# The opening loads of a cross-covariance attention and MLP kernel: the first chunks of k and q in two half transfers, the second chunks over GpSimd's queue

## The chip, the cores and the metric

The kernel runs on one core of one Trainium2 chip; the other cores are idle. Its time is the device time of one execution in microseconds (us), the median of several runs. A core has five engines that run side by side: TensorE (PE, matrix multiply), VectorE (DVE), ScalarE (ACT), GpSimd (POOL) and SyncE (SP). SP, ACT and POOL can also issue DMA transfers; each has a queue of its own, and all queues are served by the same 16 DMA engines.

## The reference

Inputs are q, k and v, each of shape (4, 6080, 256) in float32, and the weights of an MLP. For each of the four batches:

```python
qn = q / (np.linalg.norm(q, axis=1, keepdims=True) + 1e-06)
kn = k / (np.linalg.norm(k, axis=1, keepdims=True) + 1e-06)
s = kn.transpose(0, 2, 1) @ qn / tau        # 256 x 256
a = softmax(s)                              # over the last axis
x = v @ a
h = x @ w_in                                # 256 -> 2048
r = np.maximum(h, 0.0)
out = (s_moe * (r * r) + b_moe) @ w_out     # 2048 -> 256
```

The output is 24320 x 256 in float32. The sum over the 6080 rows has to be complete before the softmax of a batch can be taken, so no output row of a batch can be computed before all of that batch's k and q have been read.

## The kernel before

**The two parts.** For each batch the kernel forms the Gram matrix of q and k (256 x 256, in the PSUM tile `s_ps`, line 148), the column sums of squares of k and q (`n_ps`, lines 246 and 250), from these the softmax (`eT`, line 302), and folds the softmax into w_in (`wa`, lines 323 to 332). Then groups of 512 tokens run through the MLP: `mm1` (line 755), relu, square, and the second product (lines 802, 830 and 926). For batches 1 to 3 the first part is spread over the steps of the MLP of the batch before, so it runs beside other work. For batch 0 there is nothing to run beside: this is the opening of the kernel, about its first 37 us, and the change is in it.

**The opening.** The rows of k and q of batch 0 are cut into 13 chunks: 11 of 512 rows (128 partitions, 4 rows each, 512 KB in float32 for k and the same for q), one of 256 rows and one of 192. A chunk's tile `qk` holds both in float16. There are two ways into it:

- The first `NDIRECT` = 2 chunks come as float32 over the queues of SP (k) and ACT (q) into `raw32` (line 130), and are then cast into `qk` by DVE (k, line 138) and ACT (q, line 139).
- The other chunks come over GpSimd's queue (line 132), whose transfers cast to float16 on the way. The pool `qk_pool` has 8 buffers, and a transfer of this queue waits until the one issued eight transfers earlier has landed.

The loads are issued in the order of the chunks (lines 498 to 510): k and q of each, for the last three chunks (`NLATE` = 3) first all of k and then all of q. After them on GpSimd's queue come the first rows of v, the weights, and so on.

**The work on a chunk.** TensorE does 8 matmuls of 128x256 for a chunk (line 148), which need k and q. ACT squares k, and q of odd chunks (line 179); DVE squares q of even chunks (line 176) and folds the squares into one running sum (lines 193 and 207). After some chunks TensorE also does one or two matmuls on constant data whose result nobody reads:

```python
FILL = {-8: 1, -7: 1, -6: 1, -5: 2, -4: 2}   # key: chunk minus 13
def keep_busy(n):
    for _ in range(n):
        po(nc.tensor.matmul(h_tile("idle_ps")[:, 0, :], fill[:, :P], fill, ...
```

So chunks 5, 6 and 7 are followed by one such filler and chunks 8 and 9 by two. For the last three chunks the order is another: first the squares and the norm of k, then ACT's four steps from the sum of squares to 1/norm (line 271), and beside them the squares, norms and matmuls of q. Then `scale`, the exponentials, and the first block of `wa`, after which the first matmul of line 755 can start.

**What sets the order.** Nearly every instruction goes through `po`, which keeps it in the order of the program on its engine; so the order on each engine is that of the source. The transfers of line 130 are not under `po`, but in the compiled program they are the first that SP and ACT issue.

Of the kernel before, what the change touches and what calls it, by code (L numbers as in the profile page):

```python
# [16 lines left out]
def kernel(  # L17
# [12 lines left out]
    nc = tc.nc  # L30
    P = 128
# [23 lines left out]
    def po(ins):  # L55

        tc.keep_in_program_order(ins)
        return ins
# [34 lines left out]


    JC = 4
    NDIRECT = 2

    def make_chunks(rows_of):
        chunks, at = [], 0
# [11 lines left out]
    class Gram:  # L111
# [7 lines left out]
        def load(self, c, parts=(0, 1)):  # L119

            at, np_, jc = self.chunks[c]
            if 0 in parts:
                self.raw[c] = qk_pool.tile([P, 2, JC, C], FP16, tag="qk", name="qk")
            t = self.raw[c]
            direct = self.b == 0 and c < NDIRECT
            for i in parts:
                src = (k, q)[i]
                rows = src[self.b, at : at + np_ * jc, :].rearrange("(p j) c -> p j c", j=jc)
                if direct:
                    (nc.sync, nc.scalar)[i].dma_start(out=raw32[:, c, i], in_=rows)  # L130
                else:
                    po(nc.gpsimd.dma_start(out=t[:np_, i, :jc, :], in_=rows))
            self.tiles[c] = t[:, 1], t[:, 0]
# [354 lines left out]
    g0 = grams[0]  # L488
    raw32 = gpool.tile([P, NDIRECT, 2, JC, C], FP32, tag="g16", name="raw32")

# [6 lines left out]
    po(nc.vector.tensor_copy(out=ones_id, in_=fill.bitcast(FP32)[:, :P]))  # L497
    for c in range(NDIRECT):
        g0.load(c)
        g0.cast(c)  # L500
    for c in range(NDIRECT, len(g0.chunks) - NLATE):
        g0.load(c)
        if c == NDIRECT:
            po(nc.gpsimd.affine_select(
                out=ident16, in_=ones_id, compare_op=ALU.is_equal, fill=0.0, base=0,
# [156 lines left out]
    for i, f in enumerate(folds):  # L662
        early.setdefault(FOLDS[i], []).append(f)
    at_step(14, lambda: po(nc.vector.tensor_scalar_mul(
        out=s_out, in0=s_bc, scalar1=1.0 / (LAM * LAM))))
# [357 lines left out]
```

## Time and profile before

| | |
|---|---|
| time, median of 3 runs | 714.04 us (714.01 to 714.29) |
| span in the profile | 712.5 us |
| TensorE busy | 691.5 us, 97% |
| DVE, ACT, POOL busy | 635.2, 548.5, 113.4 us |
| GpSimd's DMA queue, q0 | 43.74 MB, 38.2% of 16 engines |
| SP's and ACT's queues, q1 and q10 | 37.71 MB, 21.9%; 1.25 MB, 0.5% |
| chain that ended last | PE 95%, DMA 3%, ACT 1%, DVE 1% |

The busy shares are averages over the whole span. The chain of waits starts from the last instruction and goes back, at each step, to what released it; its shares say which engine the end of the kernel hung on. In lines of the timeline the first number is the start in us from the beginning of the span, the second the length, then engine, source line, operation, what it writes and reads, and how often; in brackets stands how long the engine was idle before and what ended that. In lines of the chain there is the start, the length and the piece of work. In the DMA view one digit stands for a slice of the stretch, 9 for 90% or more of the 16 engines' time; GB/s are the bytes moved, for a casting transfer those written.

### The profile page before, as it was taken

Reading aid. Unit: us, or ns where it says so; the run is one execution under the profiler, and the core shown is the slowest. Engines: PE = TensorE matmul, PEld = TensorE weight load, DVE = VectorE, ACT = ScalarE, POOL = GpSimd, SP = SyncE. Lnnn points to the kernel's source line nnn. Section 1 sums busy time; section 2 is a strip of 40 time slices with the busy share of each in tenths; the row PEclk is TensorE's granted clock in tenths of the full one; section 3 lists DMA queues with packets and bytes.
Section 4 is the critical chain, followed back from the end, with each engine's and each line's share of the span. In section 5 each row is a group of like instructions: output and inputs, shape, how many; then the busy total and the mean of one; then the engine's idle time right before and its main releaser. Section 6 shows DMA issues by size and latency. Waiting matters only on the chain.

```text
span 712.5 us, 17529 instructions
## 1 busy us (share of the span) xinstructions
PE 691.5 (97%) x7422; PEld 501.7 (70%) x7422; DVE 635.2 (89%) x906; ACT 548.5 (77%) x599; POOL 113.4 (16%) x191
## 2 busy tenths in 40 slices
PE   4699999999999999999999999999999999999998
PEld 2456777776777777777677777777768777777777
DVE  4889999999988989998999899998998888888886
ACT  5789877787787777778877777777876777777875
POOL 4533132202101222111010222111000000000000
DMA  9999998556665878455762888737433333321202
GB/s 233 207 258 174 175 168 140 112 103 121 119 123 105 138 139 147 106 92 104 153 127 52 149 137 146 130 76 97 100 65 75 94 71 75 97 61 46 83 31 75
DMA packets 87838, 83.81 MB, mean 118 GB/s; under 512 B 56352, under 2 KB 62768, under 8 KB 87760
## 3 DMA queue, kind: packets, MB, share of 16 engines
q0 software_dynamic: 26992, 43.74, 38.2%
q1 hardware_dynamic: 60192, 37.71, 21.9%
q8 instruction: 58, 0.95, 0.6%
q10 hardware_dynamic: 576, 1.25, 0.5%
q14 instruction: 20, 0.16, 0.1%
HBM read 78.91 MB, written 24.90 MB: 146 GB/s over the span
## 4 chain that ended last, share of the span: by engine, by line
PE 95%; DMA 3%; ACT 1%; DVE 1%; issue 0%; DVEq 0%; ACTq 0%
PE h_ps L755 46%; PE o_ps L926 40%; PE s_ps L148 4%; DMA qk<-in_k_dram 1%; PE wa_ps L388 1%; DMA raw<-in_q_dram 1%; PE o_ps L830 1%; ACT sq L179 1%; PE o_ps L802 0%; PE wa_ps L330 0%; DVE f L193 0%; ACT r L271 0%; PE n_ps L246 0%; ACT qk L139 0%; DVE f L207 0%
## 5 line engine op out<-in xcount | busy, mean ns | idle before, releaser
L765 ACT ACTIVATE r<-h_ps 128x1024 f16<-128x1024 f32 (+1 forms) x384 | 388.4, 1013 | 144.2 <-PE h_ps L755 140.6
L755 PE MATMUL h_ps<-vT,wa 128*128 128x512 f16 (+7 forms) x1632 | 452.1, 364 | 0.5 <-ACT wa L323 0.5
L926 PEld LDWEIGHTS <-S 128*128 128x128 f16 x2944 | 198.1, 98 | 84.3
L926 PEld LDWEIGHTS <-g 128*128 128x128 f16 x2208 | 155.0, 98 | 74.1
L778 DVE TENSOR_TENSOR g<-r 128x2048 f16<-128x2048 f16 (+2 forms) x150 | 174.4, 1163 | 10.1 <-ACT r L765 9.7
L926 PE MATMUL o_ps<-T,S 128*128 128x128 f16 x2208 | 183.1, 219 | 0.0
L755 PEld LDWEIGHTS <-wa 128*128 128x128 f16 x1632 | 136.5, 98 | 19.0 <-ACT wa L323 1.0
L926 PE MATMUL o_ps<-w_out,g 128*128 128x128 f16 x1472 | 134.2, 219 | 0.0
L776 ACT ACTIVATE g<-r 128x1024 f16<-128x1024 f16 (+1 forms) x97 | 100.3, 1034 | 0.2
L783 DVE SCALAR_TENSOR_TENSOR o_sb<-o_ps,s_out,u 128x256 f32<-128x256 f32 x138 | 66.2, 480 | 36.1 <-PE o_ps L926 34.5
L148 PE MATMUL s_ps<-qk 128*128 128x256 f16 (+1 forms) x384 | 70.1, 283 | 16.0 <-ACT qk L139 9.3
L452 POOL DMA_DIRECT2D v<-in_v_dram x48 | 31.3, 661 | 241.1 <-DMA vT<-v 165.1
L209 POOL DMA_DIRECT2D f<-f x33 | 28.8, 874 | 245.6 <-DVE f L193 202.8
L783 DVE SCALAR_TENSOR_TENSOR u<-o_ps,s_out,rowconst 128x256 f32<-128x256 f32 x138 | 65.7, 476 | 0.0
L926 PE MATMUL o_ps<-w_out,S 128*128 128x128 f16 x736 | 63.5, 219 | 0.0
L926 PE MATMUL o_ps<-N,g 128*128 128x128 f16 x736 | 63.4, 219 | 0.0
L855 DVE TENSOR_TENSOR S<-S,g 128x2048 f16<-128x2048 f16 (+1 forms) x47 | 56.4, 1201 | 1.2
L179 ACT ACTIVATE sq<-qk 128x1024 f16<-128x1024 f16 (+2 forms) x53 | 54.5, 1041 | 3.9 <-DMA qk<-in_k_dram 2.3
L853 DVE TENSOR_TENSOR S<-g 128x2048 f16<-128x2048 f16 (+1 forms) x47 | 56.0, 1192 | 0.0
L857 DVE TENSOR_TENSOR S<-g 128x2048 f16<-128x2048 f16 x46 | 55.8, 1214 | 0.0
L859 DVE TENSOR_TENSOR S<-g,S 128x2048 f16<-128x2048 f16 x46 | 55.8, 1214 | 0.0
L148 PEld LDWEIGHTS <-qk 128*128 128x128 f16 (+1 forms) x384 | 32.2, 101 | 21.4 <-ACT qk L139 9.8
(103 smaller groups left out, 333.6 us busy)
## 6 DMA issues: line engine op xcount, KB each, us to landing
out_dram<-o_sb SPq DMA_DIRECT2D x43, 512.0 KB, 2.9
v<-in_v_dram POOLq DMA_DIRECT2D x47, 256.0 KB, 4.8
qk<-in_k_dram POOLq DMA_DIRECT2D x42, 256.0 KB, 6.5
qk<-in_q_dram POOLq DMA_DIRECT2D x42, 256.0 KB, 7.5
f<-f POOLq DMA_DIRECT2D x30, 128.0 KB, 3.1
vT<-v SPq DMA_TRANSPOSE x182, 3.2
w<-in_moe_w_out_dram POOLq DMA_DIRECT2D x4, 512.0 KB, 9.8
out_dram<-o_sb SPq DMA_DIRECT2D x8, 256.0 KB, 5.1
```

What stands on the lines that cost most here:

```text
L148: po(nc.tensor.matmul(self.s_ps[:, ch, :], qc[:np_, j, ts(ch, P)], kc[:np_, j, :], start=(c == 0 and j == 0 and ch == 0), stop=(c == len(s ...
L179: po(nc.scalar.activation(out=st["sq"][:np_, a, js, :], in_=(qc, kc)[a][:np_, js, :], func=AF.Square))
L755: po(nc.tensor.matmul(dst, wa[:, ci, ts(m, P)], src, start=(ci == 0), stop=(ci == CH - 1), skip_group_check=True))
L765: po(nc.scalar.activation(out=r16[:, :, i % 2, :n], in_=h_tiles.pop((g, i))[:, :, :n], func=AF.Relu))
L776: po(nc.scalar.activation(out=dst, in_=src, func=AF.Square))
L778: po(nc.vector.tensor_mul(dst, src, src))
L783: po(nc.vector.scalar_tensor_tensor(out=dst, in0=src, scalar=s_out, op0=ALU.mult, in1=add, op1=ALU.add))
L853: po(nc.vector.tensor_add(T[1], A21, A22))
L855: po(nc.vector.tensor_sub(T[2], T[1], A11))
L857: po(nc.vector.tensor_sub(T[3], A11, A21))
L859: po(nc.vector.tensor_sub(T[4], A12, T[2]))
L926: po(nc.tensor.matmul(st[name][:, j, :], a()[:, i, ts(j, P)], w[:, i, :], start=first, stop=last, skip_group_check=True))
```

## The change

`NDIRECT` goes from 2 to 1, so only chunk 0 still takes the way over `raw32`, and chunk 1 goes over GpSimd's queue with its cast on the way. The transfers of chunk 0 are cut into two of 64 partitions each, one behind the other on SP's queue for k and on ACT's for q. It is for having the first data early with less in front of it, and for taking the casts of chunk 1 off DVE and ACT.

```diff
-    NDIRECT = 2
+    NDIRECT = 1
...
                 if direct:
-                    (nc.sync, nc.scalar)[i].dma_start(out=raw32[:, c, i], in_=rows)
+                    for h in range(2):
+                        ps = ts(h, P // 2)
+                        (nc.sync, nc.scalar)[i].dma_start(out=raw32[ps, c, i], in_=rows[ps])
                 else:
                     po(nc.gpsimd.dma_start(out=t[:np_, i, :jc, :], in_=rows))
```

In the compiled program TensorE, DVE, ACT and SP keep their order. DVE and ACT each lose one cast (lines 138 and 139), SP and ACT issue two transfers of 64 x 1024 in place of two of 128 x 1024, and GpSimd issues two more of 128 x 1024, chunk 1 now being the first on its queue. The semaphores that GpSimd's transfers report to are counted on by two places.

## The prediction

> **What bounds the kernel now.** I read the page first (engine shares, slices, chain), then the chain of the opening in order of time, then the DMA view and TensorE's timeline of the opening alone. TensorE is busy 97% of the span and the chain is 95% TensorE, so from about 37.5 us to the end an edit to two early loads can't do more than shift everything. The opening is different. The chain of waits from 26 to 38 us:
>
> ```profile
> 20.68 9.46 DMA qk<-in_k_dram
> 30.13 0.02 issue
> 30.16 1.07 ACT sq L179
> 31.22 0.02 issue
> 31.25 0.44 DVE half L223
> 31.68 0.04 issue
> 31.73 0.95 PE n_ps L246 x7
> 32.68 0.02 issue
> 32.70 0.48 ACT r L271
> ```
>
> The reader sees that the first matmuls of the output (L755, 37.49 us) hang on the landing of k's chunk 10 at 30.13 us, and then on a string of short steps with no slack. What sets that landing is the DMA view of 10 to 30 us (slices of 0.5 us; GB/s counts the written fp16, so bytes read are twice that):
>
> ```profile
> DMA  9999999999999999999999999999999999999999
> GB/s 209 213 217 201 205 213 209 213 209 205 213 209 205 213 205 213 209 209 213 205 209 209 213 209 209 209 205 213 213 209 205 201 217 217 205 209 201 217 197 197
> ...
> q0 software_dynamic: 2372, 4.17, 112.4%
> ```
>
> All 16 engines are full, by GpSimd's queue (q0) alone: 4.17 MB written, 8.34 MB read in 20 us, 417 GB/s. k and q of batch 0 are 2 x 6080 x 256 x 4 B = 12.45 MB, that is 29.9 us at this rate, counted back from a last landing of about 32.5 us or a little later. So the opening is a stream of a fixed number of bytes, and its end depends on when the engines fill up and on nothing else. TensorE's timeline of the opening shows the pace:
>
> ```profile
> 7.45 1.89 PE L148 MATMUL s_ps<-qk 128*128 128x256 f16 x8 [7.45 <-ACT qk L139]
> 11.24 1.04 PE L148 MATMUL s_ps<-qk 128*128 128x256 f16 x4 [1.90 <-ACT qk L139]
> ```
>
> ```profile
> 11.24 4.66 PE L148 MATMUL s_ps<-qk 128*128 128x256 f16 x24 [1.90 <-ACT qk L139]
> 16.38 1.05 PE L148 MATMUL s_ps<-qk 128*128 128x256 f16 x8 [0.48 <-DMA qk<-in_q_dram]
> 18.93 1.05 PE L148 MATMUL s_ps<-qk 128*128 128x256 f16 x8 [1.51 <-DMA qk<-in_q_dram]
> ...
> 26.40 1.05 PE L148 MATMUL s_ps<-qk 128*128 128x256 f16 x8 [1.17 <-DMA qk<-in_q_dram]
> 27.20 0.71 PE L548 MATMUL idle_ps<-fill 128*128 128x512 f32 x2
> 28.95 1.05 PE L148 MATMUL s_ps<-qk 128*128 128x256 f16 x8 [1.04 <-DMA qk<-in_q_dram]
> ```
>
> Chunk 0 runs at 7.45. Chunk 1 waits for its casts until 11.24, and by then chunks 2 and 3 are in, so three chunks run as one block of 24. From chunk 4 on, each waits for its own q, 2.51 us apart ((28.95 - 16.38) / 5). TensorE, DVE and ACT are behind at 11 us and have caught up by 17.
>
> **What the Trainium skill says.** "DMA: Bandwidth & Descriptors", section "Rules for kernel authors": two transfers to the two partition halves serialise, since both spray across all 16 engines, and spreading issues over SP, ACT and GpSimd brings no bandwidth. The trace can't show halves; on spreading it agrees: with three queues at work (5.4 to 9.8 us) 1.44 MB were written, 0.39 of them cast, so 1.83 MB read in 4.4 us, 416 GB/s against 417 later with one queue. The same page, "Why a DMA increments its semaphore by 16 and not by 1": the engines used are the largest number up to 16 that divides the slowest dimension, so 64 partitions still use 16. No trace here shows it; I rely on it. Same page, "Queues, rings and completion order": an engine goes round-robin between its rings. It agrees: of 5.4 to 9.8 us SP's ring had about 0.49 MB, ACT's 0.56 and GpSimd's read 0.78. "TensorE: Matmul & The Clock Gate", Part 1: TensorE runs at half clock until some 3.4 us of sustained activity, in free-running windows. It agrees: the 8 matmuls of chunk 0 start (1.89 - 0.42) / 7 = 0.21 us apart (0.42 is the length of one there), those of chunk 4 (1.05 - 0.27) / 7 = 0.11. In the block of 24, 23 steps take 4.66 - 0.27 = 4.39 us, which is 18 at 0.213 and 5 at 0.109: the clock rose about 3.85 us after 11.24.
>
> **The change, part by part.**
> (1) Chunk 0 in halves: still two issues on SP and two on ACT (0.40 to 0.45 us each, the same count as the two whole chunks of before), the same 1.05 MB, the same casts, which wait for both halves. Bounds: if a half's issue takes half as long, 0.2 us are gained on the second half; if each transfer had its own ramp, 0.2 to 0.4 us lost on chunk 0. Both only move chunk 0's landing (6.17 and 6.35 us now), which nothing at 30 us waits for. I take 0.
> (2) Chunk 1 goes over q0: two DMA instructions more on GpSimd (0.53 to 0.58 us each, beside a stream that takes 1.25 us per transfer: hidden), and one cast less on DVE (0.69 us) and ACT (1.04). Those two engines wait for DMA from 17 us on, so 0 at the end.
> (3) When the engines are full. By 5.4 us SP's and ACT's rings had moved 0.56 + 0.49 = 1.05 MB, just the size of chunk 0, and q0 its first packet at 5.45, though issued at 1.30. In the changed kernel the two rings hold only chunk 0, so they run dry just when q0 starts. Is there a hole? By the packet records chunk 0's transfers end on the 16 engines between 4.98 and 5.96 us, and q0's first packets follow in the same order of engines, 0.5 to 0.6 us behind each: they look held by their turn, not by arrival. With an empty queue later in the kernel, v's loads show 0.8 to 1.24 us from issue to first packet. If they are held by turn, no hole; if 5.45 is the arrival, up to 0.46 us on the fastest engine and none on the slowest, which ends at 5.96 and alone decides a landing. I take 0, bound +0.46.
> (4) Depth. q0 keeps 8 transfers in flight: each issue waits for the one 8 before. With two more at the head, chunk 8's k still waits for chunk 4's k, chunk 10's k for chunk 6's: the later waits are the same, renumbered, and what is queued behind them on GpSimd moves with them. Only chunk 5 now waits for chunk 1 (about 8 us), with seven transfers (8.8 us of work) before it: hidden.
> (5) Rate: 1.05 MB read through q0 instead of mixed rings: 417 against 416 GB/s, 0.01 us.
> (6) TensorE's pattern. The n-th transfer of 512 KB lets its matmuls start at 16.38 - 1.255 x (10 - n). So chunk 1 (n = 4) can run at 8.85, chunk 2 at 11.36, chunk 3 at 13.87. At half clock a chunk takes 8 x 0.213 = 1.71 us: 7.45 to 9.16, 9.16 to 10.87, 11.36 to 13.07, 13.87 to 15.58. The block of 24 is gone, so the clock may rise later. Up to chunk 7 that costs nothing: 1.71 plus a filler of 0.43 is 2.14 of 2.51 us. Chunks 8 and 9 with two fillers are 2.56 each, so TensorE is busy without a break from 26.40 to 31.5 and the clock should be up by 30 to 33. Cost 0 if up by 31.7.
>
> Sum: 0 + 0 + 0 + 0 + 0 + 0, so 714.0 us, the present median, and nothing after 37.5 us changes.
>
> **The rivals.**
> A, slower: the half clock lasts into the late phase. For it: the lost block; the fillers were sized for an array already at speed. Against: 5.1 us without a break just before. If it lasts until about 33.2, the 7 norm matmuls from 31.73 take 1.49 in place of 0.95 us and chunk 10 begins 0.67 us late: 714.7. If it lasts through, chunks 10 to 12 and q's norms add to 37.5 in place of 34.92: +2.6, 716.6.
> B, faster: the engines fill earlier. First data is at 1.83 us and the slices reach full rate near 4. The 1.05 MB of 5.4 us are worth 2.5 us at 417 GB/s, an effective start of 2.9; perfect from 1.83 would be 1.1 us better, 712.9, the ceiling. The spread of 0.98 us between engines lasts; halves could even it out: half of it is 0.5 us, 713.5. Against: nothing in the change shortens the first packet's way.
> C: a hole or a slower ramp by smaller transfers, the bounds of (1) and (3): +0.5, 714.5.
>
> **How the numbers follow.** No change within 0.4 us: 0.67. A: 0.11 at 714.7 and 0.05 at 716.6. B: 0.12, of which 0.03 beyond what I reckon and past 0.2%. C: 0.05. The limit of 0.2% is 1.43 us: below 712.6 only the tail of B (0.03, and 0.01 for what I don't see), above 715.5 only the worse half of A (0.05, and 0.03 for what I don't see). Range 713.4 to 715.0: it takes in A's likelier value, most of B and C, and leaves out A's worse value, B's end and the unseen, about 0.15.
>
> **What would show it.** Right: chunk 1's matmuls start near 9 and not at 11.24 and its cast is gone; q0 runs from about 5 us or before with the DMA slices full; chunks 4 to 9 start within 0.3 us of 16.38 to 28.95; chunk 10's k lands within 0.4 us of 30.13; L755 starts within 0.4 us of 37.49; the L148 matmuls of chunk 10 are 0.11 us apart. Wrong: those matmuls at 0.21 us apart (A); an empty slice between 4 and 7 us with all landings later (C); landings all earlier by over 0.5 us (B); or a difference that arises after 38 us, which none of my steps has.

## The result, and the profile after

| | before | after |
|---|---|---|
| time, median of 22 runs each | 714.11 us (713.79 to 714.39) | 715.19 us (714.96 to 715.99) |
| ratio, 95% interval | | 1.0016 (1.001 to 1.0023) |
| ACT starts the square of k's chunk 10 | 30.16 us | 31.25 us |
| first matmul of line 755 (757 after) | 37.49 us | 38.66 us |

The changed kernel is 1.1 us slower; the forecast was no change, in a range that ended at 715.0. Line numbers from the loads on are two higher after the change. The chain of waits of the changed kernel from 20 to 40 us:

```profile
21.77 9.46 DMA qk<-in_k_dram
31.22 0.02 issue
31.25 1.07 ACT sq L181
...
32.81 0.95 PE n_ps L248 x7
...
33.79 0.48 ACT r L273
...
38.66 0.61 PE h_ps L757 x2
```

The reader sees the same chain with the same lengths, every piece 1.1 us later (the first matmul 1.17; the two profiled runs, 715.36 and 714.21 us, are 1.15 apart). Nothing is added behind the landing of k's chunk 10, so the loss lies before it. The DMA view of the changed kernel from 10 to 30 us:

```profile
DMA packets 2301, 4.19 MB, mean 209 GB/s; under 512 B 256, under 2 KB 256, under 8 KB 2301
...
q0 software_dynamic: 2301, 4.19, 112.2%
```

That is the rate of before (4.17 MB). So the loss is older than 10 us. The view of 4 to 9 us has it. A queue's line gives its packets, the MB written, and the time that the packets took as a share of 16 engines' time. First the kernel before:

```profile
DMA  9998999989999899999999999999999999999999
...
DMA packets 558, 1.84 MB, mean 367 GB/s; under 512 B 50, under 2 KB 50, under 8 KB 558
...
q10 hardware_dynamic: 224, 0.83, 40.7%
q1 hardware_dynamic: 212, 0.77, 39.1%
q0 software_dynamic: 122, 0.24, 25.7%
```

and the changed kernel:

```profile
DMA  9499999999999999999999969799699899999998
...
DMA packets 477, 1.13 MB, mean 226 GB/s; under 512 B 73, under 2 KB 73, under 8 KB 477
...
q0 software_dynamic: 282, 0.53, 56.9%
q10 hardware_dynamic: 115, 0.34, 32.0%
q1 hardware_dynamic: 80, 0.26, 18.6%
```

q0 reads twice what it writes, so before 1.84 + 0.24 = 2.08 MB were read in these 5 us, after 1.13 + 0.53 = 1.66. The 0.42 MB that are missing take 1.0 us at 417 GB/s: the whole loss. Yet the slices are nearly full in both, and the three queues' shares add up to 105.5% before and 107.5% after (a sum past 100% means that the times of packets overlap). What differs is what a packet costs: ACT's queue, q10, had 40.7% of 16 engines for 0.83 MB before, 32.0% for 0.34 MB after. Per packet of 4096 B that is 0.407 x 16 x 5 us / 0.83 MB x 0.0041 MB = 0.16 us before and 0.31 us after; for q1 0.17 and 0.23. q0's packets stay at 0.175. SP's and ACT's queues together moved 1.60 MB for 79.8% of the engines before and 0.60 MB for 50.6% after, that is about 60% as much in the same busy time. A full slice is no proof of a full rate.

TensorE's timeline of the changed kernel:

```profile
10.52 6.25 PE L150 MATMUL s_ps<-qk 128*128 128x256 f16 x32 [10.52 <-ACT qk L141]
17.55 1.05 PE L150 MATMUL s_ps<-qk 128*128 128x256 f16 x8 [0.79 <-DMA qk<-in_q_dram]
...
22.57 1.82 PE L150 MATMUL s_ps<-qk 128*128 128x256 f16 x8 [1.28 <-DMA qk<-in_q_dram]
...
25.01 1.55 PE L150 MATMUL s_ps<-qk 128*128 128x256 f16 x8 [0.20 <-DMA qk<-in_q_dram]
...
27.58 1.05 PE L150 MATMUL s_ps<-qk 128*128 128x256 f16 x8 [0.78 <-DMA qk<-in_q_dram]
...
30.02 1.05 PE L150 MATMUL s_ps<-qk 128*128 128x256 f16 x8 [0.92 <-DMA qk<-in_q_dram]
```

Chunk 0, meant to come early, starts at 10.52 in place of 7.45 us: its casts begin at 8.91 and 9.42 us, where they began at 6.17 and 6.35. Chunks 0 to 3 then run as one block of 32. The clock falls back to half in chunks 6 and 7 (1.82 and 1.55 us long, at 22.57 and 25.01), and is up again by chunk 8 (27.58).

### The profile page after: what moved, and what is told of

Its sections match the earlier page's. It is cut to its first block, busy times and chain, and to the rows that moved or that the text cites. A ratio compares the mean times of both kernels' runs of the same rounds, so it can differ in the third digit from the quotient of the medians.

```text
span 713.7 us, 17531 instructions
## 1 busy us (share of the span) xinstructions
PE 692.8 (97%) x7422; PEld 502.5 (70%) x7422; DVE 634.7 (89%) x905; ACT 547.9 (77%) x598; POOL 114.5 (16%) x193
## 4 chain that ended last, share of the span: by engine, by line
PE 95%; DMA 4%; ACT 1%; issue 0%; DVE 0%; POOL 0%; ACTq 0%; POOLq 0%
PE h_ps L757 46%; PE o_ps L928 40%; PE s_ps L150 5%; DMA qk<-in_q_dram 2%; DMA qk<-in_k_dram 1%; PE wa_ps L390 1%; PE o_ps L832 1%; PE o_ps L804 0%; PE wa_ps L332 0%; ACT r L273 0%; PE n_ps L248 0%; ACT sq L181 0%; POOL qk L134 0%; ACT eT L304 0%; PE vT_ps L465 0%
```

## The experiments

Three theories stand against each other. P says that transfers into part of the partitions are slow themselves, T that every transfer more costs a start of its own, and S that moving chunk 1 to GpSimd's queue does the harm. "Behind" below is how much later than in the profile of the kernel before 10 MB of k and q had been read, worked out from the packet records of the two traces; "chunk 10" is ACT's start on k's chunk 10 (30.16 us before). Diffs are against the changed kernel. The time of the kernel before that stands beside a run was taken together with that run.

**Chunk 0 whole.**

```diff
-                    for h in range(2):
-                        ps = ts(h, P // 2)
-                        (nc.sync, nc.scalar)[i].dma_start(out=raw32[ps, c, i], in_=rows[ps])
+                    (nc.sync, nc.scalar)[i].dma_start(out=raw32[:, c, i], in_=rows)
```

> Chunk 0 in one transfer of 128 partitions per queue again, chunk 1 stays on GpSimd's queue. Theory P (the halves are the cause: a transfer into 64 partitions is written at about half the rate, its packets take some 300 ns in place of 160): the loss goes away, 713.9 to 714.4 us, k's chunk 10 lands at 30.0 to 30.4 us, packets of SP's and ACT's queues near 160 ns. Theory T (each transfer more on a queue costs a start of its own, about 1 us after the one before, whatever its shape): the same, since two transfers fewer. Rival S (the cause is chunk 1 on GpSimd's queue: the two fast queues run dry and GpSimd's starts late): 715.0 to 715.4 us, chunk 10 at 31.2.

Measured: 714.32 us against 713.97, ratio 1.0003 (0.9995 to 1.0011), 0.17 us ahead, chunk 10 at 30.05. S falls. Its TensorE timeline is the one that the prediction wrote for the change:

```profile
7.40 3.35 PE L148 MATMUL s_ps<-qk 128*128 128x256 f16 x16 [7.40 <-ACT qk L139]
11.27 1.05 PE L148 MATMUL s_ps<-qk 128*128 128x256 f16 x8 [0.52 <-DMA qk<-in_q_dram]
13.81 1.89 PE L148 MATMUL s_ps<-qk 128*128 128x256 f16 x8 [1.50 <-DMA qk<-in_q_dram]
16.28 1.89 PE L148 MATMUL s_ps<-qk 128*128 128x256 f16 x8 [0.58 <-DMA qk<-in_q_dram]
```

Chunks 0 and 1 in one piece, chunk 2 at 11.27, chunk 3 at 13.81 (worked out: 11.36 and 13.87).

**Halves alone, chunk 1 direct as before.**

```diff
-    NDIRECT = 1
+    NDIRECT = 2
...
-                    for h in range(2):
-                        ps = ts(h, P // 2)
+                    for h in range(2 if c == 0 else 1):
+                        ps = ts(h, P // 2) if c == 0 else slice(0, P)
```

> Chunk 0 in two half transfers per queue, chunk 1 whole and direct on SP's and ACT's queues as before the change. P and T: the loss stays, 714.8 to 715.4 us, and the half transfers' packets are again near 300 ns. S: no loss, 713.9 to 714.4 us.

Measured: 716.79 us, ratio 1.0044 (1.0031 to 1.0056), 1.59 us behind; packets of 4 to 9 us at 0.28 us on q1 and 0.31 on q10. Worse than expected, because a second bound comes up. From its chain:

```profile
2.32 10.96 DMA raw<-in_q_dram
13.30 1.04 ACT qk L141
...
31.07 0.70 DVE f L195
31.79 0.44 DVE f L195
32.25 0.42 DVE f L209
...
34.13 1.65 PE n_ps L248 x7
```

q's chunk 1 lands at 13.28, and from there on the chain is ACT's cast and squares up to 17.2 us and then DVE's squares and folds without a gap, up to k's norms at 34.13. In the kernel before DVE was busy for 13.5 of the 15 us from 16 to 31; it can't make good a start this late. Also, in this profiled run the norm matmuls take 1.65 in place of 0.95 us: TensorE is at half clock there, my rival A. That run took 718.5 us, the others 716.5 to 716.9.

**Cut by rows: two transfers per queue, each to all 128 partitions.**

```diff
-                        ps = ts(h, P // 2)
-                        (nc.sync, nc.scalar)[i].dma_start(out=raw32[ps, c, i], in_=rows[ps])
+                        js = ts(h, JC // 2)
+                        (nc.sync, nc.scalar)[i].dma_start(out=raw32[:, c, i, js], in_=rows[:, js])
```

> As the change, but chunk 0 is cut by rows: each of the two transfers per queue goes to all 128 partitions, with 2 of 4 rows (2 KB in place of 4 KB). Same number of transfers, same bytes each. P: no loss, 713.9 to 714.4 us. T: the loss of the change, 714.9 to 715.4 us. S: 715.0 to 715.4 us.

Measured: 713.99 us against 713.97, ratio 1.0003 (0.9995 to 1.0011), 0.23 us ahead, chunk 10 at 29.86. As many transfers and bytes as in the change, and no loss: T falls, and P stands.

**Which side of the transfer.** In a half transfer the changed kernel reads one block of 256 KB and writes one block of 64 partitions. Three variants take every second piece in place of a block, on the side of the target, of the source, or of both. Both first:

```diff
-                        ps = ts(h, P // 2)
+                        ps = slice(h, P, 2)
```

> As the change, but one transfer takes the even and the other the odd partitions, so each has 64 partitions spread over the whole memory. P with the limit in which part of the memory is written: no loss, 713.9 to 714.4 us, packets near 160 ns. T: the loss of the change, 714.9 to 715.4 us. A variant of P in which 64 descriptors as such are slow: the loss stays too, with packets near 300 ns.

Target a block, source every second row of 4 KB:

```diff
-                        ps = ts(h, P // 2)
-                        (nc.sync, nc.scalar)[i].dma_start(out=raw32[ps, c, i], in_=rows[ps])
+                        (nc.sync, nc.scalar)[i].dma_start(
+                            out=raw32[ts(h, P // 2), c, i], in_=rows[slice(h, P, 2)])
```

> Halves again, one behind the other: the target is a half of the partitions in one block, the source every second 4 KB piece of the whole 512 KB (k and q alike, so the sums over rows are the same). If the block of partitions makes the packets slow: near 300 ns as in the change, loads 1.0 us behind, 714.9 to 715.4 us. If reading one block of 256 KB does: near 160 ns, loads 0.7 us behind, 714.6 to 715.1.

Target every second partition, source a block:

```diff
-                        ps = ts(h, P // 2)
-                        (nc.sync, nc.scalar)[i].dma_start(out=raw32[ps, c, i], in_=rows[ps])
+                        (nc.sync, nc.scalar)[i].dma_start(
+                            out=raw32[slice(h, P, 2), c, i], in_=rows[ts(h, P // 2)])
```

> The mirror: the target is every second partition, the source one block of 256 KB. If the block of partitions makes the packets slow: near 160 ns, loads 0.7 us behind. If the block read does: near 300 ns, loads 1.0 us behind.

| target | source | time, before beside it | ratio (interval) | behind | chunk 10 |
|---|---|---|---|---|---|
| block | block (the change) | 715.19, 714.11 | 1.0016 (1.001 to 1.0023) | 1.01 us | 31.25 |
| block | every second | 715.57, 714.04 | 1.0021 (1.0013 to 1.003) | 1.19 us | 31.24 |
| every second | block | 714.08, 714.04 | 1.0000 (0.9991 to 1.0008) | 0.16 us | 29.97 |
| every second | every second | 715.00, 713.97 | 1.0014 (1.0007 to 1.002) | 0.71 us | 30.70 |

The DMA view of 4 to 9 us, target a block and source spread:

```profile
DMA packets 478, 1.18 MB, mean 237 GB/s; under 512 B 69, under 2 KB 69, under 8 KB 478
...
q0 software_dynamic: 260, 0.49, 54.1%
q10 hardware_dynamic: 137, 0.43, 32.9%
q1 hardware_dynamic: 81, 0.26, 15.3%
```

and target spread, source a block:

```profile
DMA packets 581, 1.35 MB, mean 270 GB/s; under 512 B 79, under 2 KB 79, under 8 KB 581
...
q0 software_dynamic: 378, 0.71, 75.5%
q10 hardware_dynamic: 123, 0.38, 19.9%
q1 hardware_dynamic: 80, 0.26, 14.3%
```

1.18 + 0.49 = 1.67 MB read in the first, as in the change, against 1.35 + 0.71 = 2.06 in the second, as before it. q10's packets take 0.25 us in the first and 0.17 in the second. So it is the target in one block of partitions that makes the difference: with the source a block, as in the change, spreading the target alone takes the slow packets and the loss away. That run issues its first transfers as slowly as the change (0.58 us), has its first data as late (2.17 us), and costs nothing that the time shows. Two queues at once aren't needed for the slow packets: from 3.5 to 4.2 us in the changed kernel q's first half is all but alone, its packets take 101.1% of the 16 engines' time (k's take 2.9%), and it moves 0.16 MB, that is 0.23 MB per us where the full stream reads 0.417. But not every packet into a block is slow: 44 of the 64 packets of k's first half in the change took 0.16 to 0.18 us, and with the source spread k's second half took 0.19 us a packet on average, where q's took 0.28.

The source has a share of its own: spreading it adds 0.18 us to "behind" with the target in a block and 0.55 with the target spread, the latter with packets at 0.18 us. So its cost is not a slow packet, and the traces show where it arises. From 3 to 5 us the packets take only 0.72 of the 16 engines' time with the target in a block and 0.69 with both sides spread, against 1.05 in the change and 0.97 with only the target spread. By 5 us the two runs with a spread source have read 0.62 and 0.64 MB, where the kernel before had read 0.88: 0.6 us at 417 GB/s in both. The 0.71 us of the run with both sides spread are thus nearly all a stretch of partly idle engines, and of the 1.19 us with the target in a block about half are; only the rest is slow packets. Why the engines are not full there isn't shown. My expectations had no such stretch: the run with both sides spread has the time that T gave it and the packets that P gave it, the run with a block as target and a spread source came out above its 1.0 us and 715.4, and for the spread target with a block as source I had taken those 0.71 us for the price of a late start, so that 0.7 us was too high.

**Quarters, and unequal parts.**

```diff
-                    for h in range(2):
-                        ps = ts(h, P // 2)
+                    for h in range(4):
+                        ps = ts(h, P // 4)
```

> As the change, but chunk 0 in four transfers of 32 partitions per queue. If narrow transfers into one block of partitions are slow in themselves, their packets take some 600 ns in place of the 300 of the halves and 160 of whole ones; if each start also costs, the last of chunk 0 lands past 11 us. The loss at least doubles: 716 to 719 us; DVE, late with its first chunk, may become the bound of the opening, as in the run with chunk 1 direct. If packets stay at 300 ns and the time at 715.2, the width isn't the cause.

```diff
-                    for h in range(2):
-                        ps = ts(h, P // 2)
+                    for ps in (slice(0, 96), slice(96, P)):
```

> Chunk 0 in transfers of 96 and 32 partitions. If any second transfer to part of the partitions costs what the halves cost: 714.9 to 715.4 us. If the width of the first counts: issued in about 0.4 us as the whole and the quarter are, first data near 1.85 us and packets near 160 ns for the 96, so the loads fall behind by less than 0.6 us and the time is 714.1 to 714.7.

Quarters: 716.13 us against 714.02, ratio 1.0031 (1.002 to 1.0042), 0.96 us behind, chunk 10 at 32.24; packets of q10 and q1 at 0.30 and 0.28 us. 96 and 32: 715.55 against 714.04, ratio 1.0022 (1.0013 to 1.0031), 0.64 behind, chunk 10 at 31.56; packets at 0.28 and 0.26. The second is above both of the times that I had expected. The loss doubles with quarters, but the packets do not take 0.6 us: half the width does not double them again, so "rate in proportion to the partitions" is not the rule. Both runs also clear the long issue: the first transfer of a queue takes 0.57 to 0.59 us to issue where it has 64 partitions, and 0.39 to 0.41 where it has 128, 96 or 32, and first data comes at 2.16 us in place of 1.84. The quarters and the 96 lose without it, the spread target had it and lost nothing.

In both runs chunk 10 lands later than "behind" says, by 1.1 and 0.8 us. "Behind" is a mean over 16 engines, and the landing is that of one transfer. Some engines may have been further behind than the mean; that was not worked out engine by engine.

**Only k in halves.**

```diff
-                    for h in range(2):
-                        ps = ts(h, P // 2)
+                    for h in range(2 if i == 0 else 1):
+                        ps = ts(h, P // 2) if i == 0 else slice(0, P)
```

> Only k's chunk 0 in halves; q's in one transfer of 128 partitions. If each half transfer costs on its own account: half the loss, 714.4 to 714.8 us, the stream of loads 0.3 to 0.6 us behind the kernel before. If the loss comes only from both queues being narrow at the same time: 713.9 to 714.3.

Measured: 715.27 us against 714.02, ratio 1.002 (1.001 to 1.003), 0.41 behind, chunk 10 at 30.86; q1's packets at 0.31 us. By bytes half the loss, as expected; but chunk 10 lands 0.70 us late, and the time, above the 714.4 to 714.8 expected, is that of the whole change. The run isn't simply one half of the change: k's first packet came at 3.56 us, where it came at 2.16 in the change. Between the profiled runs (715.18 us, and 714.21 before) the first matmul of line 757 explains 0.72 of 0.97 us; where the rest arises I can't say.

**TensorE's clock.**

```diff
-    FILL = {-8: 1, -7: 1, -6: 1, -5: 2, -4: 2}
+    FILL = {-9: 2, -8: 2, -7: 2, -6: 2, -5: 2, -4: 2}
```

> The changed kernel with two fillers behind each of chunks 4 to 9, so that TensorE's clock stays up from chunk 4 on. My rival A of the prediction (the half clock in the late phase) expects 714.0 to 714.4 us. The theory that the loads alone are late expects no change: 714.9 to 715.4.

Measured: 716.07 us, ratio 1.0028 (1.0017 to 1.0039). The mean granted clock is 1.000 in all seven runs (0.998 in the change's profile), and the kernel isn't faster but 0.9 us slower than the change, outside both expectations. So rival A had no part in the change's loss: the half clock is gone and the loss isn't. Where the 0.9 us come from is to be seen on DVE (33 to 36 us), the changed kernel first:

```profile
33.70 1.57 DVE L178 TENSOR_TENSOR sq<-qk 128x1024 f16<-128x1024 f16 x3 [0.27 <-DMA qk<-in_q_dram]
```

```profile
33.85 1.05 DVE L178 TENSOR_TENSOR sq<-qk 128x1024 f16<-128x1024 f16 x2 [0.26 <-DMA qk<-in_q_dram]
35.79 0.42 DVE L178 TENSOR_TENSOR sq<-qk 96x512 f16<-96x512 f16 x1 [0.89 <-DMA qk<-in_q_dram]
```

q's last chunk lands about 0.9 us later. The DMA view of this kernel from 33 to 36 us has a packet that the changed kernel has only at 36.6:

```profile
q8 instruction: 1, 0.02, 2.0%
```

That is one fetch of instructions, 16 KB, 0.97 us on one of the 16 engines. With 12 fillers in the program in place of 7 it falls due 2.8 us earlier, in front of the last load. That it causes the delay is read from the trace; the first of the two tries below shows the same once more.

**Two tries at a better kernel,** both cut by rows: with two fillers behind each of chunks 1 to 9, and with the same seven fillers as before, one behind each of chunks 3 to 9. Their edits beside the cut by rows, the first and the second:

```diff
-    FILL = {-8: 1, -7: 1, -6: 1, -5: 2, -4: 2}
+    FILL = {-12: 2, -11: 2, -10: 2, -9: 2, -8: 2, -7: 2, -6: 2, -5: 2, -4: 2}
```

```diff
-    FILL = {-8: 1, -7: 1, -6: 1, -5: 2, -4: 2}
+    FILL = {-10: 1, -9: 1, -8: 1, -7: 1, -6: 1, -5: 1, -4: 1}
```

> Cut by rows over 128 partitions as in the run before, with two fillers behind every chunk from 1 to 9: the version that could beat the kernel before, since its loads were 0.2 us ahead and its first casts and matmuls earlier. If the clock cost it something, 713.6 to 713.8 us; if not, 713.8 to 714.1, which can't be told from before.

> Chunk 0 cut by rows over all 128 partitions, with the same seven fillers as before the change, but one behind each of chunks 3 to 9: the number of instructions stays, so no fetch of instructions moves into the loads, and the clock should stay up from chunk 3 on. If the loads' lead of 0.2 to 0.3 us counts at the end: 713.6 to 713.8 us. If not: 713.9 to 714.1, no better than before the change.

The first took 714.72 us against 714.02 (1.0013, 1.0006 to 1.0019). Its 21 runs fall in two groups: 15 at 714.5 to 715.2 with a mean clock of 1.000, six at 715.9 to 716.1 with 0.998. The profiled one is of the six:

```profile
33.08 1.91 PE L150 MATMUL s_ps<-qk 128*128 128x256 f16 x8
```

Chunk 10 at half clock: rival A as I described it, at about 1.3 us a time. The other 15 runs, still some 0.7 us slower than the cut by rows, were not profiled. The profiled run shows a likely reason: with 18 fillers the fetch of instructions comes at 30.07 us, and DVE, after a wait of 0.68 us, squares k's last chunk at 32.11, where it did so at 31.29 in the cut by rows (fetch at 35.06). The second try has 7 fillers, and its fetch is at 35.04. The second took 714.43 against 714.01 (1.001, 1.0003 to 1.0016), between 713.9 and 716.7. Neither beats the kernel before, though their loads were 0.15 to 0.17 us ahead, and neither reached its expectation. No version tried beats it.

## Why the prediction was wrong, point by point

- **The bound.** Right. The chain kept its shape, and 1.09 us at the landing of chunk 10 came out as 1.08 us in the time.
- **(1), the halves: the step that failed.** I bounded their cost at 0.2 to 0.4 us and said it moves only chunk 0's landing, "which nothing at 30 us waits for". That was the error: the half transfers don't wait in the background, they occupy all 16 engines at up to twice the price, and what they lose is lost to the whole stream behind them. Chunk 0's casts came 2.7 and 3.1 us late, which indeed cost nothing on the chain; the stream fell 1.0 us behind, which cost all of it. What the Trainium skill says in "DMA: Bandwidth & Descriptors", section "Why a DMA increments its semaphore by 16 and not by 1", of 16 engines for 64 partitions agrees: the trace shows 16 busy engines, by q's first half alone from 3.5 to 4.2 us (101.1%). That the rate stays whole when the number of engines does was my own inference, and the trace denies it (0.31 in place of 0.16 us a packet on ACT's queue). The same page's advice (Rules for kernel authors), one transfer of 128 partitions in place of two halves, holds here.
- **(2), chunk 1 on GpSimd's queue.** Right: with chunk 0 whole no loss clear of the noise.
- **(3), a hole.** Right that there is none to speak of: the slices of 4 to 9 us are nearly full, and q0's first packet came at 4.26 us, earlier than the 5.45 of before, so 5.45 was not its arrival.
- **(4) and (5), depth and rate.** Right: 4.19 against 4.17 MB in 10 to 30 us.
- **(6), TensorE.** The times were right for chunk 0 whole. In the change its late chunk 0 made a block of 32; the clock did fall back, in chunks 6 and 7, and was up in time, at no cost.
- **The rivals.** C (0.05) comes nearest to what happened, but in half: the smaller transfers did cost, at twice the 0.5 us that I gave them, yet not by a hole or a slower ramp, and the sign that I named for C, an empty slice between 4 and 7 us, isn't there. No rival had slow packets on full engines. B didn't come. A was not at work in the change, as more fillers showed, but it is real, in the run with chunk 1 direct and in the first try at a better kernel.

What makes a target in one block of partitions slow no run here shows, and it stays open: that quarters are no slower per packet than halves speaks against a plain share of the memory's width. Also open are why the engines are not full with a spread source, and the long issue of 64 partitions. Sending the halves in opposite order on the two queues was not tried.

## What to carry to other kernels

When a stream of loads is the bound, price a change of a transfer's shape by the time that its packets hold the engines, not by when it lands: a full slice says that the engines are busy, and bytes per busy time say whether they are fast. To cut a load in two, cut it along the rows inside the partitions: here that cost nothing. A target spread over the partitions cost nothing only where the source stayed a block; with even and odd partitions and their own rows the kernel lost almost as much as with halves (1.0014 against 1.0016). Take late first work on a busy engine as a second bound, and check the landings themselves as well as the bytes, since the two disagreed by up to 1.1 us here.

## What the runs showed of the hardware

- Packets of 4096 B from 4 to 9 us took 0.16 to 0.17 us into all 128 partitions and 0.17 to 0.18 into every second one. Into one block they took 0.23 and 0.31 us on the two queues (64 partitions, the change), 0.28 and 0.30 (32 partitions), 0.26 and 0.28 (parts of 96 and 32). With a spread source it was 0.19 and 0.25 (64 partitions). The first half of k in the change was an exception: 44 of its 64 packets took 0.16 to 0.18 us.
- With a source of every second row of 4 KB, the 16 engines were only 0.69 to 0.72 busy from 3 to 5 us, against 0.97 to 1.05 with a source in one block.
- Issuing a first transfer of 64 partitions took 0.57 to 0.59 us, one of 32, 96 or 128 took 0.39 to 0.41.
- A fetch of instructions is a packet of 16 KB that takes 0.97 us of one DMA engine. It was seen at 36.6 us in the change with 7 fillers and at 33.75 with 12; cut by rows, at 35.06 with 7 and at 30.07 with 18. In both longer programs a load close behind it came 0.8 to 0.9 us late.
- TensorE's half clock in the opening can differ from run to run of one program: of 21 runs 15 had a mean granted clock of 1.000 and six one of 0.998, about 1.3 us slower.
